# A Fourier filter and a two-layer block on one core: who begins stage one's stores, when the transform's steps are issued, and who casts the filtered product

## The chip, the cores and the metric

The kernel runs on one core of one Trainium2 chip. The metric is the device time of one execution in microseconds (us), the median of several runs.

## The reference, cut to what matters

```python
# x 8 x 3008 x 256, filt_r and filt_i 1505 x 256, w_in 256 x 2048, w_out 2048 x 256, all fp32
X = np.fft.rfft(x, axis=1)
y = np.fft.irfft(X * (filt_r + 1j * filt_i), n=3008, axis=1)
t = y.reshape(24064, 256)
h = t @ w_in
g = h * (1.0 / (1.0 + np.exp(-1.702 * h)))
out = g @ w_out
```

Each of the 8 batches goes through a Fourier transform of length 3008, a product with a filter and the transform back; its 3008 tokens then go through two matrix products with a gelu between them.

## The kernel before, in words

**Two jobs run side by side.** The two matrix products (the MLP, `mlp`, L590) of batch b keep TensorE busy; between their matmuls the transform of batch b + 1 (`fft`, L439) is done. The first transform is done alone ahead of everything, by other code that the change leaves alone. So there are seven transforms beside MLPs: the "first transform" below is the one of batch 1, done beside the MLP of batch 0; the last batch's MLP runs alone.

**The MLP.** A batch has six tiles of tokens, 512 wide; the sixth of batches 0, 2, 4 and 6 is 384 wide, since what is left over goes to the next batch. A tile has 16 chunks, one for each 128 of the 2048 middle columns, so a batch has 96 chunks. A chunk is 6 matmuls into h (L603: values are split into a high and a low part, and three products of the parts are taken, for two halves of the inner dimension) and 6 into o (L625). Between them ScalarE takes the gelu of h rounded (gh, L606) and again unrounded in place (h, L607), and VectorE takes the difference (gl, L608). gh and gl have three buffers each, h two. When a tile is done ScalarE and VectorE copy o out (L631, L634) and SyncE begins the store (L644).

**The transform, stage one** is 12 steps, two halves u of six chunks c. SyncE begins the load of x (512 KB, L444, by the helper at L182); per half ScalarE casts the high part xh (L449), GpSimd takes the low part xl (L450), TensorE does three matmuls (L279 to L281), ScalarE casts ah (L454), VectorE takes al (L455). After the second half four stores of 256 KB each (L460) bring ah and al to DRAM (a_d). x, ah, al, and later b and br, share one pool of seven buffers ("raw"), so the load of x for chunk c + 2 takes the buffer that al of chunk c - 1 leaves when its stores have landed.

**Stage two** is two empty steps and then 17 pairs, a forward step i (L493) and a backward step i - 1 (L511). Forward: two matmuls s from zy (L483 to L488), which GpSimd has loaded from a_d (L469); ScalarE copies one half and VectorE adds the other (L436, L437); VectorE multiplies by the filter (L427 to L429) and GpSimd adds (L430); then the sum c_buf is split again: VectorE casts the high part into zy (L504, twice, 48 x 512) and GpSimd takes the low part (L505, twice). Backward: two matmuls i, the halves again, and two stores of b to DRAM (b_d, L520), begun by ScalarE. From b_d come the loads br (SyncE, L182) for the last piece, which makes the tile's y: eight matmuls (L576), ScalarE's cast (L584) and VectorE's difference (L585).

**What sets the order.** The main loop (L684 to L720) walks over the chunks; behind each chunk's work it issues steps of the next transform. There are 48 calls for a batch, spread evenly over its chunks by count: the k-th is issued when 48 x chunk // chunks reaches k, where chunks is 86 (the last ten chunks of a batch get none; in batch 0 the first 16 don't either, so it is 70). The last ones are needed before the next batch's first tile is made. From the code as issued, a scheduler with a simulated clock sets the order of instructions on each engine. Each engine then runs its list strictly in that order, and a DMA is begun by the engine named, in that engine's order: a DMA that waits holds up what stands behind it there.

Of the kernel before, what the change touches and what calls it, by code (L numbers as in the profile page):

```python
# [20 lines left out]
P = 128  # L21
Q = 112
NFC = DFF // P
STEPS = 48

LEAST = 2.0**-15
MOST = float(np.uint32(0x47EFFFFF).view(np.float32))
# [125 lines left out]
def tile_kernel(  # L153
# [9 lines left out]
    nc = tc.nc  # L163
# [8 lines left out]
    def raw(name):  # L172
        return sb.tile([P, 4, D], F32, tag="raw", name=name, bufs=7)
# [6 lines left out]
    def load_in(dst, src):  # L180

        ins = nc.sync.dma_start(dst, src)  # L182
        if in_order[0]:
            tc.keep_in_program_order(ins)
# [254 lines left out]
    def fft(b):  # L439

        a_d = dram.tile([2, 48, 64, D], F32, tag="a_d", name=f"a_d{b}")
        for c in range(6):
            xr = raw(f"x_{b}_{c}")
            load_in(xr, x[b, c])  # L444
            ah, al = (sb.tile([P, 4, D], F32R, tag="raw", name=f"a{n}_{b}_{c}", bufs=7) for n in "hl")
            for u in range(2):
                xh, xl = half(f"xh_{b}_{c}_{u}"), half(f"xl_{b}_{c}_{u}")
                src = xr[:, 2 * u : 2 * u + 2, :]
                nc.scalar.copy(xh, src)  # L449
                nc.gpsimd.tensor_tensor(xl, src, xh.bitcast(F32), ALU.subtract)  # L450
                ps = ps_f.tile([P, 2, D], F32, tag="f", name=f"s1_{b}_{c}_{u}")
                mm3(ps, t1_sb[:, 0], t1_sb[:, 1], xh, xl)
                su = slice(2 * u, 2 * u + 2)
                nc.scalar.copy(ah[:, su], ps)  # L454
                nc.vector.tensor_tensor(al[:, su], ps, ah[:, su].bitcast(F32), ALU.subtract)  # L455
                yield
            for j in range(2):
                n = NH * j + 4 * c
                for k, a in enumerate((ah, al)):
                    nc.scalar.dma_start(  # L460
                        a_d[k, n : n + 4].rearrange("n k d -> k n d"), a[64 * j : 64 * j + 64].bitcast(F32)
                    )

        b_d = dram.tile([48, 64, D], F32, tag="b_d", name=f"b_d{b}")

        def load(i):
            for k in range(2):
                src = a_d[k].rearrange("n (k s) d -> n k s d", k=2)[:, :, 2 * i : 2 * i + 2, :]
                nc.gpsimd.dma_start(  # L469
                    zy[0][64 * k : 64 * k + 48, i % 2].rearrange("p k s d -> p k (s d)"),  # L470
                    src.rearrange("n k s d -> n k (s d)"),
                )

        def load_f(i):
            for k in range(2):
                load_in(f_buf[64 * k : 64 * k + 48, 2 * (i % 2) : 2 * (i % 2) + 2], fs[i])

        def second(i, m, src, name):

            ps = [ps_f.tile([P, 2, D], F32, tag="f", name=f"{name}_{b}_{i}_{k}") for k in range(2)]  # L480
            for k in range(2):
                if i == 0:
                    ins = nc.tensor.matmul(ps[k][:, 0], de_sb[:, k, m + 1], src[:, k, 0], start=True, stop=True)  # L483
                    if k == 0:
                        tc.keep_in_program_order(ins)
                    nc.tensor.matmul(ps[k][:, 1], de_sb[:, k, m], src[:, k, 1], start=True, stop=True)
                else:
                    ins = nc.tensor.matmul(ps[k], de_sb[:, k, m], src[:, k], start=True, stop=True)  # L488
                    if k == 0:
                        tc.keep_in_program_order(ins)  # L490
            return ps

        def forward(i):  # L493

            ps = second(i, 0, zy[0][:, i % 2], "s2")
            if i + 2 < 16:
                load(i + 2)
            u1 = c_buf[i % 3]
            halves(ps, u1)
            product(i, u1, u1, f_buf[:Q, 2 * (i % 2) : 2 * (i % 2) + 2])  # L500
            y = zy[0][:, 2 + i % 2]
            for k in range(2):
                h, o = slice(64 * k, 64 * k + 48), slice(64 - 64 * k, 112 - 64 * k)
                nc.vector.tensor_copy(y[h, k], u1[h])  # L504
                nc.gpsimd.tensor_tensor(y[o, k], u1[h], y[h, k].bitcast(F32), ALU.subtract)  # L505
            if i + 2 < 16:
                load_f(i + 2)

        bes = {}

        def backward(i):  # L511
            g, u = divmod(i, 2)
            if u == 0:
                bes[g] = raw(f"b_{b}_{g}")
            ps = second(i, 2, zy[0][:, 2 + i % 2], "i2")
            halves(ps, bes[g][:Q, 2 * u : 2 * u + 2, :])
            if u == 1:
                be = bes.pop(g)
                for k in range(2):
                    nc.scalar.dma_start(b_d[:, 32 * k + 4 * g : 32 * k + 4 * g + 4, :], be[64 * k : 64 * k + 48])  # L520

        for i in range(2):
            load(i)
            load_f(i)

        for i in range(2):
            yield
        for i in range(17):
            if i < 16:
                forward(i)  # L530
                yield
            if i:
                backward(i - 1)
                yield
        b_of[b] = b_d
# [148 lines left out]
    for n, (i, fc) in enumerate(turns):  # L684
        b, t = tiles[i]
        if n % (6 * NFC) == 0:

            lead = 16 if b == 0 else 0
            done, chunk, chunks = 0, 0, 6 * NFC - lead - 10
            nxt = fft(b + 1) if b + 1 < B else iter(())  # L690
        if n == 0:
            run(start(*tiles[1]))
        if n + 1 < len(turns):
            ahead(*turns[n + 1])
        chunks_of[i][1](fc, turns[n + 1 : n + 2] == [(i, fc + 1)])
        if fc == 1:
            store()
        if n < 26:
            run(conv, 1)
            if n % 2 and n < 12:  # L700
                load_unit(EARLY + 9 + n // 2)
        if n == 11:
            split_de()
            in_order[0] = False
        if n == 26:
            zy.append(const.tile([P, 4, 2, 2, D], F32R, tag="zy", name="zy"))
            nc.gpsimd.memset(zy[0].bitcast(F32), 0.0)
        if b or n >= lead:
            chunk += 1
            while chunk <= chunks and done < STEPS * chunk // chunks:  # L710
                run(nxt, 1)
                done += 1
        at = () if i == 0 else (10, 11, 13) if i == 1 else (9, 12, 13) if t == 5 else (1, 3, 9)
        if fc in at and i + 1 < len(tiles):
            if i + 1 not in sigs:
                sigs[i + 1] = start(*tiles[i + 1])
            run(sigs[i + 1], 1)
            if fc == at[-1]:
                run(sigs[i + 1])
# [29 lines left out]
```

## Time and profile before

| what | value |
|---|---|
| three runs | 2384.24, 2385.23, 2387.87 us; median 2385.23 |
| the profiled execution | 2385.31 us, of which the profile's span is 2383.5 and 1.8 lie around it |
| TensorE | 2365.1 us busy, 99% of the span, 11102 matmuls |
| VectorE, ScalarE, GpSimd | 59%, 55%, 30% busy |
| TensorE's granted clock | full speed in every slice |

PE is TensorE, DVE VectorE, ACT ScalarE, POOL GpSimd, SP SyncE; a q behind a name is the engine's sequencer, which issues DMAs. The span is the profiled execution on the chip; busy time doesn't count the issuing of DMAs. Matmuls overlap and their ends are modelled, so the distance between starts is the safer reading: a matmul of 512 columns starts every 0.227 us. The difference between span and busy time of TensorE, 18.4 us, is all the idle time that the trace shows for it.

### The profile page before, as it was taken

To read this page: it belongs to the slowest core of one execution; us is meant where nothing else is said; L and a number is where in the kernel's file an instruction comes from. 1 tells how busy PE (TensorE), PEld (TensorE's weight loads), DVE (VectorE), ACT (ScalarE), POOL (GpSimd) and SP (SyncE) were. 2 spreads that over 40 slices of the span, in tenths; PEclk is the share of its full clock that TensorE was granted. 3 is DMA by queue.
4 is the path that set the end of the run, shared out by engine and by line. 5 is a ranking of instruction groups with operands and counts; after the bars stand their busy time and mean duration, and the time that the engine had idled before them with its cause. 6 is when DMAs were issued, how large, how long until landed. Compare 5 with 4: busy or idle time off the path is not lost.

```text
span 2383.5 us, 31272 instructions
## 1 busy us (share of the span) xinstructions
PE 2365.1 (99%) x11102; PEld 1984.1 (83%) x11102; DVE 1411.2 (59%) x2199; ACT 1314.4 (55%) x2430; POOL 724.9 (30%) x675
## 2 busy tenths in 40 slices
PE   9999999999999999999999999999999999999999
PEld 7878888888888889888888888988888888898887
DVE  7967873577535774367743677437773377723222
ACT  6655655566555565555645556555654555644443
POOL 3024532344213441244412444124440144300000
PEclk9999999999999999999999999999999999999999
DMA  9255534544245442544425444354433544220000
GB/s 343 81 149 116 119 93 116 142 107 111 54 128 135 104 111 80 139 109 111 99 81 133 110 109 102 93 138 108 119 89 87 133 108 120 75 64 9 18 9 18
DMA packets 141483, 248.66 MB, mean 104 GB/s; under 512 B 15376, under 2 KB 81040, under 8 KB 141328
## 3 DMA queue, kind: packets, MB, share of 16 engines
q1 hardware_dynamic: 63088, 136.18, 19.6%
q10 hardware_dynamic: 53152, 66.44, 11.0%
q0 software_dynamic: 25088, 44.05, 9.6%
q8 instruction: 88, 1.44, 0.3%
q14 instruction: 67, 0.55, 0.1%
HBM read 152.76 MB, written 93.85 MB: 103 GB/s over the span
## 4 chain that ended last, share of the span: by engine, by line
PE 92%; DVE 3%; DMA 2%; issue 1%; ACT 1%; ACTq 0%; POOL 0%; SPq 0%; POOLq 0%; DVEq 0%
PE h L603 41%; PE o L625 41%; PE i L576 3%; PE i L488 2%; PE s L488 2%; PE s L279 1%; PE s L281 1%; PE s L280 1%; DVE u_buf L427 1%; PE s L358 1%; DVE u_buf L428 0%; DVE gl L608 0%; DMA x<-in_x_dram 0%; DVE c_buf L437 0%; DMA zy<-a_d 0%
## 5 line engine op out<-in xcount | busy, mean ns | idle before, releaser
L603 PE MATMUL h<-y,wi 128*128 128x512 f32 (+1 forms) x4608 | 1156.7, 386 | 5.7 <-DVE gl L608 5.6
L603 PEld LDWEIGHTS h<-y,wi 128*128 128x128 f32 x4608 | 854.9, 188 | 172.5 <-DVE gl L608 11.5
L608 DVE TENSOR_TENSOR gl<-h,gh 128x512 fp32r<-128x512 f32 (+1 forms) x768 | 522.3, 680 | 759.3 <-ACT h L607 746.4
L606 ACT ACTIVATE gh<-h 128x512 fp32r<-128x512 f32 (+1 forms) x768 | 453.1, 590 | 783.2 <-PE h L603 756.6
L625 PE MATMUL o<-gh,wo 128*128 128x512 f32 (+1 forms) x3072 | 821.3, 387 | 2.6 <-ACT gh L606 2.5
L625 PEld LDWEIGHTS o<-gh,wo 128*128 128x128 f32 x3072 | 569.9, 188 | 111.9 <-ACT gh L606 4.9
L625 PE MATMUL o<-gl,wo 128*128 128x512 f32 (+1 forms) x1536 | 472.5, 385 | 0.0
L607 ACT ACTIVATE h<-h 128x512 f32<-128x512 f32 (+1 forms) x768 | 448.2, 584 | 0.0
L505 POOL TENSOR_TENSOR zy<-c_buf,zy 48x512 fp32r<-48x512 f32 x224 | 314.5, 1404 | 84.0 <-DVE zy L504 74.8
L625 PEld LDWEIGHTS o<-gl,wo 128*128 128x128 f32 x1536 | 286.9, 188 | 54.9 <-DVE gl L608 0.2
L430 POOL TENSOR_TENSOR c_buf<-c_buf,u_buf 112x512 f32<-112x512 f32 x127 | 163.6, 1288 | 395.3 <-DVE c_buf L429 395.3
L450 POOL TENSOR_TENSOR xl<-x,xh 128x512 fp32r<-128x512 f32 x84 | 108.8, 1303 | 548.9 <-ACT xh L449 543.3
L469 POOL DMA_DIRECT2D zy<-a_d x224 | 129.8, 581 | 271.0 <-PE s L488 92.5
L437 DVE TENSOR_TENSOR c_buf<-s,c_buf 48x512 f32<-48x512 f32 x224 | 154.3, 689 | 33.2 <-ACT c_buf L436 28.3
L437 DVE TENSOR_TENSOR b<-i,b 48x512 f32<-48x512 f32 x224 | 154.1, 688 | 9.1 <-ACT b L436 3.6
L436 ACT COPY b<-i 48x512 f32<-48x512 f32 x224 | 130.4, 582 | 47.1 <-PE i L488 37.6
L436 ACT COPY c_buf<-s 48x512 f32<-48x512 f32 x224 | 130.5, 582 | 44.7 <-PE s L488 37.2
L576 PEld LDWEIGHTS i<-tab,br 128*128 128x128 f32 x768 | 103.1, 191 | 10.4 <-issue 1.2
L504 DVE CAST zy<-c_buf 48x512 fp32r<-48x512 f32 x224 | 96.8, 432 | 22.3 <-POOL c_buf L430 14.7
L576 PE MATMUL i<-tab,br 128*128 128x128 f32 x768 | 104.4, 274 | 1.2 <-DMA br<-b_d 1.0
L455 DVE TENSOR_TENSOR al<-s,ah 128x512 fp32r<-128x512 f32 x84 | 58.0, 690 | 69.8 <-ACT ah L454 67.6
L585 DVE TENSOR_TENSOR y<-i,y 128x512 fp32r<-128x512 f32 (+2 forms) x104 | 65.2, 632 | 40.3 <-ACT y L584 39.4
(94 smaller groups left out, 1155.0 us busy)
## 6 DMA issues: line engine op xcount, KB each, us to landing
f_buf<-fs SPq DMA_DIRECT2D x224, 192.0 KB, 3.2
zy<-a_d POOLq DMA_DIRECT2D x224, 192.0 KB, 3.6
x<-in_x_dram SPq DMA_DIRECT2D x47, 512.0 KB, 4.9
out_dram<-out SPq DMA_DIRECT2D x43, 512.0 KB, 3.6
a_d<-ah ACTq DMA_DIRECT2D x84, 256.0 KB, 3.7
a_d<-al ACTq DMA_DIRECT2D x84, 256.0 KB, 4.0
b_d<-b ACTq DMA_DIRECT2D x112, 192.0 KB, 2.5
br<-b_d SPq DMA_DIRECT2D x84, 256.0 KB, 4.4
```

Source lines behind the costliest of these rows:

```text
L430: eng.tensor_tensor(u1, u1, u2, ALU.add)
L436: nc.scalar.copy(dst[h], ps[k][o])
L437: nc.vector.tensor_tensor(dst[h], ps[k][h], dst[h], ALU.add)
L450: nc.gpsimd.tensor_tensor(xl, src, xh.bitcast(F32), ALU.subtract)
L469: nc.gpsimd.dma_start(zy[0][64 * k : 64 * k + 48, i % 2].rearrange("p k s d -> p k (s d)"), src.rearrange("n k s d -> n k (s d)"),)
L505: nc.gpsimd.tensor_tensor(y[o, k], u1[h], y[h, k].bitcast(F32), ALU.subtract)
L576: ins = nc.tensor.matmul(ps[:, P * i : P * i + P], br[m][:, i], t2_sb, start=True, stop=True)
L603: nc.tensor.matmul(ps[:, :w], wi_sb[half][:, wk, kc, c], y[:, yk, kc, :w], start=n == 0, stop=n == 5)
L606: nc.scalar.activation(gh[:, :w], ps[:, :w], AF.Gelu_apprx_sigmoid)
L607: nc.scalar.activation(ps[:, :w], ps[:, :w], AF.Gelu_apprx_sigmoid)
L608: nc.vector.tensor_tensor(gl[:, :w], ps[:, :w], gh[:, :w].bitcast(F32), ALU.subtract)
L625: nc.tensor.matmul(pos[m][:, :w], wb[:, P * m : P * m + P], g[:, :w], start=first_one, stop=last_one)
```

## The change

Three things are changed.

The four stores of a chunk of stage one (L460) are begun by SyncE instead of ScalarE.

The steps of the transform get a cost each, instead of all counting the same: 0.8 for each of the 12 of stage one, 1.3 for the two empty ones, 1.0 for the other 33, in sum 45.2. The chunks get a weight too, 4 for a chunk of a 512-wide tile and 3 for one of a 384-wide tile, and the last ten units of four get no step as before. A step is issued when the costs up to and with it are no more than the passed share of the weights. By this rule, in the MLPs of batches 1, 3 and 5 the last step of stage one is issued at chunk 19 (before at 22), the first forward step at 26 (27) and the last step at 86 (85); in those of batches 2, 4 and 6 the last step comes at chunk 83 instead of 85.

The cast of the filtered product's high part (L504) goes from VectorE to ScalarE.

```diff
--- before.py
+++ after.py
@@ -21,7 +21,7 @@
 P = 128
 Q = 112
 NFC = DFF // P
-STEPS = 48
+COSTS = [0.8] * 12 + [1.3] * 2 + [1.0] * 33
 
 LEAST = 2.0**-15
 MOST = float(np.uint32(0x47EFFFFF).view(np.float32))
@@ -457,7 +457,7 @@
             for j in range(2):
                 n = NH * j + 4 * c
                 for k, a in enumerate((ah, al)):
-                    nc.scalar.dma_start(
+                    nc.sync.dma_start(
                         a_d[k, n : n + 4].rearrange("n k d -> k n d"), a[64 * j : 64 * j + 64].bitcast(F32)
                     )
 
@@ -501,7 +501,7 @@
             y = zy[0][:, 2 + i % 2]
             for k in range(2):
                 h, o = slice(64 * k, 64 * k + 48), slice(64 - 64 * k, 112 - 64 * k)
-                nc.vector.tensor_copy(y[h, k], u1[h])
+                nc.scalar.copy(y[h, k], u1[h])
                 nc.gpsimd.tensor_tensor(y[o, k], u1[h], y[h, k].bitcast(F32), ALU.subtract)
             if i + 2 < 16:
                 load_f(i + 2)
@@ -686,7 +686,9 @@
         if n % (6 * NFC) == 0:
 
             lead = 16 if b == 0 else 0
-            done, chunk, chunks = 0, 0, 6 * NFC - lead - 10
+            widths = [3 if k // NFC == 5 and b % 2 == 0 else 4 for k in range(lead, 6 * NFC)]
+            passed, whole = 0, sum(widths) - 40
+            steps, spent = list(COSTS), 0.0
             nxt = fft(b + 1) if b + 1 < B else iter(())
         if n == 0:
             run(start(*tiles[1]))
@@ -706,10 +708,10 @@
             zy.append(const.tile([P, 4, 2, 2, D], F32R, tag="zy", name="zy"))
             nc.gpsimd.memset(zy[0].bitcast(F32), 0.0)
         if b or n >= lead:
-            chunk += 1
-            while chunk <= chunks and done < STEPS * chunk // chunks:
+            passed += widths.pop(0)
+            while steps and spent + steps[0] <= sum(COSTS) * passed / whole + 0.01:
                 run(nxt, 1)
-                done += 1
+                spent += steps.pop(0)
         at = () if i == 0 else (10, 11, 13) if i == 1 else (9, 12, 13) if t == 5 else (1, 3, 9)
         if fc in at and i + 1 < len(tiles):
             if i + 1 not in sigs:
```

SyncE in stage one of the third transform (beside the MLP of batch 1; the number behind x, ah and al is the chunk c), before:

```order
L182 DMA x_2_3618<-in_x_dram 128x1024
L182 DMA x_3_3725<-in_x_dram 128x1024
L182 DMA x_4_3830<-in_x_dram 128x1024
L644 DMA out_dram<-out_0_3805 256x1x512
L182 DMA br_2_3874<-b_d_1681 64x4x256 x2
L182 DMA x_5_3917<-in_x_dram 128x1024
```

and with the change:

```order
L182 DMA x_2_3600<-in_x_dram 128x1024
L460 DMA a_d_3424<-ah_1_3520 64x4x256 x2
L460 DMA a_d_3424<-al_1_3521 64x4x256 x2
L182 DMA x_3_3689<-in_x_dram 128x1024
L460 DMA a_d_3424<-ah_2_3602 64x4x256 x2
L460 DMA a_d_3424<-al_2_3603 64x4x256 x2
L182 DMA x_4_3771<-in_x_dram 128x1024
L460 DMA a_d_3424<-ah_3_3691 64x4x256 x2
L460 DMA a_d_3424<-al_3_3692 64x4x256 x2
L182 DMA x_5_3858<-in_x_dram 128x1024
L644 DMA out_dram<-out_0_3823 256x1x512
L460 DMA a_d_3424<-ah_4_3773 64x4x256 x2
```

Each load of x now stands behind the four stores of the chunk two before it, where before the loads followed each other; the last load has moved ahead of the tile's output store and of br.

VectorE at a forward step of stage two, before (s_2_4 is that step's matmul result, b_1 a backward step's):

```order
L428 TENSOR_TENSOR u_buf_82<-c_buf_80,f_buf 48x512
L427 SCALAR_TENSOR_TENSOR u_buf_82<-c_buf_80,f_buf 48x512
L608 TENSOR_TENSOR gl_2_9_4485<-h_2_9_4477,gh_2_9_4484 128x512
L429 TENSOR_TENSOR c_buf_80<-c_buf_80,f_buf 112x512
L608 TENSOR_TENSOR gl_2_10_4503<-h_2_10_4495,gh_2_10_4502 128x512
L504 CAST zy<-c_buf_80 48x512 x2
```

and ScalarE at a forward step with the change:

```order
L606 ACTIVATE gh_3_1_4709<-h_3_1_4702 128x512
L607 ACTIVATE h_3_1_4702<-h_3_1_4702 128x512
L520 DMA b_d_3970<-b_2_4604 48x1024
L504 CAST zy<-c_buf_79 48x512 x2
L520 DMA b_d_3970<-b_2_4604 48x1024
L606 ACTIVATE gh_3_2_4727<-h_3_2_4720 128x512
L607 ACTIVATE h_3_2_4720<-h_3_2_4720 128x512
L436 COPY c_buf_80<-s_2_7_0_4739 48x512
L436 COPY c_buf_80<-s_2_7_1_4740 48x512
L606 ACTIVATE gh_3_3_4770<-h_3_3_4763 128x512
L607 ACTIVATE h_3_3_4763<-h_3_3_4763 128x512
```

The pair of casts left VectorE, where it stood behind the next gl, and stands in ScalarE's list between pairs of gelus, here between the two stores of b.

TensorE at the end of the first transform, in the 384-wide sixth tile of batch 0 (i_1_15 is the last backward step, the second number of h the chunk of the tile), before:

```order
L488 MATMUL i_1_15_1_3139<-zy,de_sb 128x512
L625 MATMUL o_5_0_3052<-gh_5_9_3227,wo_981 128x384
L625 MATMUL o_5_1_3053<-gh_5_9_3227,wo_981 128x384
L625 MATMUL o_5_0_3052<-gh_5_9_3227,wo_981 128x384
L625 MATMUL o_5_1_3053<-gh_5_9_3227,wo_981 128x384
L603 MATMUL h_5_11_3260<-y_5_2626,wi_980 128x384 x6
```

and with the change:

```order
L488 MATMUL i_1_15_0_3083<-zy,de_sb 128x512
L603 MATMUL h_5_5_3148<-y_5_2656,wi_580 128x384 x6
L625 MATMUL o_5_0_3077<-gl_5_3_3120,wo_581 128x384
L625 MATMUL o_5_1_3078<-gl_5_3_3120,wo_581 128x384
L488 MATMUL i_1_15_1_3084<-zy,de_sb 128x512
L625 MATMUL o_5_0_3077<-gh_5_4_3137,wo_581 128x384
L625 MATMUL o_5_1_3078<-gh_5_4_3137,wo_581 128x384
L625 MATMUL o_5_0_3077<-gh_5_4_3137,wo_581 128x384
L625 MATMUL o_5_1_3078<-gh_5_4_3137,wo_581 128x384
L603 MATMUL h_5_6_3166<-y_5_2656,wi_580 128x384 x6
```

The last backward step's second matmul moved from ahead of chunk 11 of that tile to ahead of chunk 6.

## Rows read from the trace of the kernel before

**Rows 1.** The head of the page (busy us of each engine, share of the span, instructions) and, of its 40 slices, the row with TensorE's granted clock in tenths of full speed.

```profile
PE 2365.1 (99%) x11102; PEld 1984.1 (83%) x11102; DVE 1411.2 (59%) x2199; ACT 1314.4 (55%) x2430; POOL 724.9 (30%) x675
...
PEclk9999999999999999999999999999999999999999
```

**Rows 2.** The windows view: stretches of the span (us), their length, then for each engine its busy time and, in brackets, its instructions; at the end granted clock, DMA share and GB/s.

```profile
120.00:200.00 80.00, 76.27 (x349) 61.33 (x348) 51.13 (x77) 45.45 (x86) 22.66 (x20) 1.00 0.56 143
...
300.00:360.00 60.00, 55.41 (x296) 50.23 (x295) 42.32 (x67) 32.83 (x67) 23.52 (x20) 1.00 0.36 93
...
705.00:730.00 25.00, 25.00 (x116) 20.84 (x115) 9.60 (x14) 13.71 (x26) 4.39 (x4) 1.00 0.54 148
...
931.00:932.00 1.00, 0.77 (x4) 0.45 (x4) 0.00 (x0) 1.00 (x3) 1.00 (x1) 1.00 0.00 0
...
1325.00:1330.00 5.00, 3.78 (x19) 2.91 (x19) 1.98 (x3) 2.52 (x5) 1.11 (x2) 1.00 0.59 70
...
2100.00:2383.50 283.50, 278.99 (x1288) 233.44 (x1286) 79.58 (x120) 117.64 (x220) 0.53 (x2) 1.00 0.05 16
```

**Rows 3.** The waits of TensorE over the whole span: who waited for whom, us in total, times, longest.

```profile
PE h L603 <- DVE gl L608: 5.6, 9, 2.1
PE o L625 <- ACT gh L606: 2.5, 3, 2.0
PE s L483 <- DMA zy<-a_d: 2.0, 2, 1.2
...
PE i L576 <- DMA br<-b_d: 1.0, 1, 1.0
```

**Rows 4.** The first row of the waits of all engines, same columns.

```profile
ACT gh L606 <- PE h L603: 756.6, 693, 3.1
```

**Rows 5.** Groups of the page: line, engine, operation, tiles, shape, count | busy us, mean ns of one | idle time of the engine before them and what ended most of it.

```profile
L505 POOL TENSOR_TENSOR zy<-c_buf,zy 48x512 fp32r<-48x512 f32 x224 | 314.5, 1404 | 84.0 <-DVE zy L504 74.8
...
L436 ACT COPY c_buf<-s 48x512 f32<-48x512 f32 x224 | 130.5, 582 | 44.7 <-PE s L488 37.2
...
L504 DVE CAST zy<-c_buf 48x512 fp32r<-48x512 f32 x224 | 96.8, 432 | 22.3 <-POOL c_buf L430 14.7
```

**Rows 6.** The page's DMA issues: KB of one, median us from issue to landing.

```profile
x<-in_x_dram SPq DMA_DIRECT2D x47, 512.0 KB, 4.9
...
a_d<-ah ACTq DMA_DIRECT2D x84, 256.0 KB, 3.7
a_d<-al ACTq DMA_DIRECT2D x84, 256.0 KB, 4.0
```

**Rows 7.** Timeline of ScalarE in the first transform's stage one: start us, us, engine (ACTq is its sequencer issuing DMAs), line, operation, how many in a row, and idle time before with its releaser.

```profile
147.00 1.25 ACTq L460 DMA_DIRECT2D a_d<-ah  x2
148.29 1.82 ACTq L460 DMA_DIRECT2D a_d<-al  x2
150.16 0.60 ACT L606 ACTIVATE gh<-h 128x512 fp32r<-128x512 f32 x1 [3.19 <-issue]
```

**Rows 8.** Timeline of TensorE there and 11 us later, same columns.

```profile
150.81 1.19 PE L625 MATMUL o<-gh,wo 128*128 128x512 f32 x4 [2.03 <-ACT gh L606]
...
161.84 0.50 PE L279 MATMUL s<-xh,t_sb 128*128 128x512 f32 x1 [0.84 <-ACT xh L449]
```

**Rows 9.** Timeline of ScalarE in the second batch's MLP, while the third transform's stage one runs: the end of chunk 1 and the first cast of chunk 3.

```profile
389.42 0.58 ACT L454 CAST ah<-s 128x512 fp32r<-128x512 f32 x1
...
392.12 1.23 ACTq L460 DMA_DIRECT2D a_d<-al  x1
...
399.33 0.62 ACT L449 CAST xh<-x 128x512 fp32r<-128x512 f32 x1 [0.73 <-PE s L280]
```

**Rows 10.** Timeline of ScalarE, the two longest waits for an x load: one in a tile of 512 tokens, one in a tile of 384.

```profile
721.60 0.62 ACT L449 CAST xh<-x 128x512 fp32r<-128x512 f32 x1 [2.31 <-DMA x<-in_x_dram]
...
930.17 1.14 ACT L449 CAST xh<-x 128x512 fp32r<-128x512 f32 x2 [2.19 <-DMA x<-in_x_dram]
931.22 0.48 ACT L606 ACTIVATE gh<-h 128x384 fp32r<-128x384 f32 x1
```

**Rows 11.** Timeline of TensorE beside the second of them.

```profile
931.01 0.51 PE L625 MATMUL o<-gl,wo 128*128 128x384 f32 x2
931.76 0.98 PE L625 MATMUL o<-gh,wo 128*128 128x384 f32 x4 [0.23 <-ACT gh L606]
```

**Rows 12.** Timeline of VectorE near the end of the first transform.

```profile
327.83 0.69 DVE L428 TENSOR_TENSOR u_buf<-c_buf,f_buf 48x512 f32<-48x512 f32 x1
...
334.59 1.67 DVE L428 TENSOR_TENSOR u_buf<-c_buf,f_buf 48x512 f32<-48x512 f32 x1
336.28 1.65 DVE L427 SCALAR_TENSOR_TENSOR u_buf<-c_buf,f_buf 48x512 f32<-48x512 f32 x1
```

**Rows 13.** Timeline of GpSimd in the same stretch.

```profile
334.25 3.13 POOL L505 TENSOR_TENSOR zy<-c_buf,zy 48x512 fp32r<-48x512 f32 x2 [2.39 <-DVE zy L504]
```

**Rows 14.** Timeline of TensorE at chunk 32 of the third batch's MLP (the shape of it returns in each of six batches).

```profile
756.29 0.28 PE L486 MATMUL i<-zy,de_sb 128*128 128x256 f32 x1
756.89 1.45 PE L603 MATMUL h<-y,wi 128*128 128x512 f32 x5 [0.32 <-DVE gl L608]
```

**Rows 15.** Timeline of GpSimd and TensorE between stage one and stage two of the sixth transform.

```profile
1321.65 2.25 POOL L469 DMA_DIRECT2D zy<-a_d  x4 [15.02 <-issue]
...
1327.55 0.36 PE L483 MATMUL s<-zy,de_sb 128*128 128x256 f32 x1 [1.22 <-DMA zy<-a_d]
```

## The prediction

> **What bounds the kernel now.** Read the head of the page first [rows 1]: TensorE is busy for 2365.1 of 2383.5 us at full clock in every slice, with VectorE at 59%, ScalarE at 55% and GpSimd at 30%. The change adds no matmul and takes none away, so nothing can be won but TensorE's idle time, 18.4 us in all. The windows view tells where that lies [rows 2]: 80.00 - 76.27 = 3.7 us in 120 to 200 (stage one of the first transform), 60 - 55.41 = 4.6 us in 300 to 360 (that transform's end), 1.2 us in 1325 to 1330, 0.2 us at 931, and 283.50 - 278.99 = 4.5 us at the program's end, which no part of the change touches. The waits of TensorE name the releasers [rows 3]: gl of VectorE 5.6 us in 9 places, gh of ScalarE 2.5, a load of zy 2.0, a load of br 1.0. So there are a dozen short stalls, each with a cause of its own, and the sum has to be made stall by stall. The other way round, ScalarE waits 756.6 us in 693 places for TensorE's h [rows 4], 1.1 us a chunk: work that is added to or taken from ScalarE is hidden unless more than that comes at once.
>
> The whole is measured against the profiled execution, 2385.31 us, 0.08 above the median of 2385.23. About 4.8 us, 0.2%, is what a measurement can tell from no change.
>
> **Stores from SyncE: what is taken away.** In the first transform ScalarE sits in the four issues from 147.00 to 150.11 and the gh behind them begins at 150.16 [rows 7]; TensorE is idle for 2.03 us before it takes that gh [rows 8]. This stall goes: -2.0. Beside it stand 0.84 us at 161.84 for an xh that came late [rows 8] and a first wait for zy of 0.8 (the rest of the 2.0 in [rows 3], of which 1.2 is at 1327). The same group of issues in later batches, 390.0 to 393.35 [rows 9], delays no matmul: a gh can be ordered between two issues there. So 18 us of issuing that ScalarE loses per batch is worth nothing elsewhere; the cover is ScalarE's 1.1 us a chunk.
>
> The Trainium skill says in "DMA: Bandwidth & Descriptors", section "Issuing engines are not separate DMA queues", that DMAs begun by different engines run on the same 16 DMA engines, and that another issuer saves only the sequencer's time, usually small against the transfer. By that alone this term would be 0 and the whole 2 us worse. The trace disagrees here: 3.1 us of issuing made a stall of 2.03 [rows 7, 8], against a transfer of 3.7 to 4.0 us [rows 6].
>
> **Stores from SyncE: what is added.** The load of x for chunk c + 2 now stands behind four stores that wait for al of chunk c. Take chunk 1 of the third transform [rows 9]: the cast of ah ends at 390.0; four issues take 3.3 us; then x has to land. The median from issue to landing is 4.9 us [rows 6], so x is there 8.2 us after the cast; if a load alone on the queue is as quick as the stores' 3.7, 7.0. Before, x was wanted 9.3 us after that cast (399.33 - 390.00 [rows 9]). Now the steps come closer: one each 0.8 x 86 / 45.2 = 1.52 chunks instead of 86 / 48 = 1.79. At 2.72 us a chunk (12 matmuls of 0.227) that is 0.73 us per step, 1.5 us per chunk of the transform; it is wanted 7.9 us after the cast. The wait on ScalarE is so between nothing and 0.3, and where the load meets the stores' traffic, an output store or br, up to 3. What does a wait of ScalarE cost TensorE? In a 512-wide tile the longest in the trace, 2.31 us [rows 10], has no stall behind it: TensorE is busy for all of 705 to 730 [rows 2]; in a 384-wide tile 2.19 us [rows 10] costs 931.76 - 931.01 less two starts of 0.173, 0.4 us, and 0.2 in the matmuls behind it [rows 11]. I take 0.7 us for one load in each of batches 1, 3 and 5, where the steps come closest: +2.1, between 0 and 5.4 (3 x 1.8, a wait of over 3 less its cover). In the even batches the positions hardly move: 0.
>
> In the first transform's own stage one the same chain meets the tile boundary: the last x stands behind an output store, and y's cast of tile 2 stands behind xh on ScalarE, with eight matmuls waiting for it. Before, this stretch had 3.7 us of stalls [rows 2]. I put the new ones, without the 2.0 that goes, at 5.1 against 1.7, +3.4, by two more waits like the 0.84 and one of 1.7 at the boundary, an estimate between that and the 2.03. The net of the stretch is +1.4, between -2.0 and +4.
>
> **Steps by the chunks' time.** Three stalls hang on when steps come. (1) The end of the first transform, 4.6 us [rows 2]: there forward and backward steps are crowded into the narrow tile, where a chunk has 2.08 us (12 x 0.173) instead of 2.72. By the new weights the last step comes five chunks sooner, ahead of chunk 6 of that tile instead of chunk 11, and the densest part falls in 512-wide chunks. The loads br follow sooner too (1.0 of the 4.6 [rows 3]). In its place comes the first load of x of the next batch, in a narrow tile like the one at 931 [rows 10, 11]: I leave 0.8 for it and 0.4 for the rest. Net -3.4, between -4.1 and 0. (2) The stall of 1.22 us at 1327.55 for a load of zy [rows 15], whose issue on GpSimd came only at 1321.65. With stage one over three chunks sooner and the first forward step one sooner, there are two chunks, 5.4 us, more for stores and loads: -1.2, between -1.2 and 0. (3) The x wait in the narrow tiles at 931 and its like in batch 4, 0.9 together by the starts: -0.5, between -0.9 and +0.5.
>
> **The cast on ScalarE.** VectorE loses 224 casts of 432 ns, 96.8 us [rows 5]. Nearest on ScalarE is the copy of the same shape, 582 ns [rows 5]; 224 of them add 130 us to 1314, hidden under its waits for h [rows 4]. A pair takes 1.2 us in ScalarE's list between gelus, about the 1.1 us that it has free in a chunk, and far under the 2.31 that stalled nothing [rows 10]: 0, between -0.5 and the third rival's price. VectorE's relief is worth something at one place per batch: at chunk 32 the matmul behind 756.29 should start 0.12 us later, and starts 0.6 later [rows 14], for a gl that is late. At 334 to 338 one sees why: beside GpSimd's pair of L505 (3.13 us [rows 13]) VectorE's products take 1.67 and 1.65 us instead of 0.69 [rows 12]. The pair of casts ahead of them (0.87 us) is gone now, so gl comes sooner by more than the 0.5 that it was late: 6 x -0.48 = -2.9, between -2.9 and 0.
>
> **Sum.** +1.4 + 2.1 - 3.4 - 1.2 - 0.5 + 0 - 2.9 = -4.5. From 2385.3: **2380.8 us**, 0.19% less. All low ends together give -11.1 (2374), all high ends +9.9 (2395); taken as independent of each other (root of the squares of the distances) 2377 and 2387.
>
> **Rivals.** *All of it is gained.* The x chain has cover enough and the first stage one loses its 2.0 and gets nothing new: -2.0 + 0 - 4.1 - 1.2 - 0.9 + 0 - 2.9 = -11.1, 2374. For it speaks that the order was made with a simulated clock that knew of the new positions; against it, that the same clock left the stalls of before.
>
> *Given back.* The x chain costs its upper ends (+4, +5.4), the gains stand at about two thirds (-5.5): +3.9, 2389, no change that could be told. For it speaks the 7.9 us against 8.2.
>
> *The loads of x are really served after the stores: slower.* If a load on SyncE's queue starts moving only when the four stores ahead of it have, it lands 3.3 + 4.0 + 3.7 = 11.0 us after the cast [rows 6, 9], 3.1 us later than wanted. It decides from a wait of 2.3 us on [rows 10]: each of the four loads behind stores in each of six batches then costs 0.8, +19, less 8 won elsewhere: +11, 2396. Against it speaks that stores and loads of two queues overlapped so far, so that bandwidth was there; but no row has a load behind stores in one queue. The Trainium skill's page "DMA: Bandwidth & Descriptors", section "Queues, rings and completion order", says that each DMA engine takes the descriptors of a ring in ring order and goes round between rings by packets: by that rule x loses its turn beside the stores and gets one after them, which is this rival. No row of before shows it.
>
> *The cast blocks ScalarE.* It now waits for GpSimd's sum in ScalarE's own list, ahead of gh. If of the 112 forward steps each costs 0.2 us of TensorE, +22, less 8: +14, 2399. It decides where the sum is over 1.1 us late; VectorE waited there only 14.7 us in all [rows 5], which speaks against it.
>
> That the change doesn't do what it says is out: the lists of instructions show all three parts.
>
> **How the numbers follow.** Forecast (2377 to 2385) 0.42, all gained (under 2377) 0.25, given back (2385 to 2390) 0.17, loads after stores 0.10, blocked ScalarE 0.06. Half of the forecast's case lies over 0.2% under before: faster 0.21 + 0.25 = 0.46; slower, the two last rivals, 0.16; between, 0.38. The range 2373 to 2391 leaves out the two last rivals and a little below.
>
> **What would show it.** In the changed kernel's trace: no stall near 148 behind issues; SyncE's list with x about 3 us behind the first store, and ScalarE's waits for x of 0 to 3 us, with stalls of TensorE only where they pass 2.3; no stall at 1327 and none at chunk 32; the window of the first transform's end with under 2 us of idle time; ScalarE some 130 us busier, VectorE 97 less. The forecast is wrong if the waits for x pass 2.3 us in most batches (then the stores hold up the loads), or if TensorE waits for gh in many forward steps.

## The result, and the profile after

The changed kernel takes **2397.76 us** (median of 6 runs, 2396.05 to 2399.87) against 2385.44 before, a ratio of 1.0052, 95% interval 1.0039 to 1.0064. It is slower by 12.3 us; 2380.8 was forecast, with a range up to 2391. The profiled execution, one of the two longest of the six, has a span of 2397.7 us, 14.2 more than before.

Where the time went can be counted from the traces: the time from the first h matmul of one batch to that of the next (batch 0 from the span's start, batch 7 to its end), in us, here with all the experiments told below. S stands for the stores on SyncE, C for the new costs and weights, K for the cast on ScalarE. Each row but for its last column is one execution of that kernel, and one execution shows a batch to some 2 us (the last section has the reason).

| kernel | parts | 0 | 1 | 2 | 3 | 4 | 5 | 6 | 7 | span | median of runs |
|---|---|---|---|---|---|---|---|---|---|---|---|
| before | none | 361.5 | 294.8 | 286.6 | 295.2 | 287.9 | 295.1 | 286.4 | 275.9 | 2383.5 | 2385.4 |
| changed | S, C, K | 362.4 | 301.8 | 285.7 | 299.3 | 285.5 | 301.0 | 286.1 | 275.9 | 2397.7 | 2397.8 |
| E1 | C, K | 365.3 | 294.8 | 285.7 | 294.8 | 290.4 | 294.8 | 286.3 | 275.9 | 2388.0 | 2391.2 |
| E2 | S | 356.9 | 294.8 | 286.6 | 295.2 | 286.3 | 295.2 | 286.4 | 275.9 | 2377.3 | 2380.0 |
| E3 | K | 368.4 | 294.3 | 286.8 | 294.6 | 287.5 | 294.7 | 286.1 | 275.9 | 2388.3 | 2389.6 |
| E4 | C | 361.8 | 295.2 | 285.6 | 295.2 | 291.2 | 295.2 | 286.9 | 275.9 | 2387.0 | 2388.4 |
| E5 | S, K, C without the closer stage one | 362.6 | 295.2 | 285.6 | 295.2 | 285.6 | 295.2 | 285.9 | 275.9 | 2381.2 | 2383.4 |
| E6 | S, C, K, ah sooner | 361.9 | 294.9 | 285.1 | 294.9 | 287.2 | 294.8 | 286.2 | 275.9 | 2380.8 | 2384.6 |
| E7 | S, C | 358.0 | 300.6 | 285.3 | 298.7 | 285.5 | 301.3 | 287.0 | 275.9 | 2392.4 | 2394.0 |
| E8 | S, K but for the first transform | 358.4 | 295.1 | 286.7 | 294.6 | 286.2 | 294.7 | 286.1 | 275.9 | 2377.7 | 2378.2 |
| E9 | K, without its wait in the first transform | 358.4 | 294.9 | 286.6 | 295.1 | 287.3 | 294.6 | 286.1 | 275.9 | 2378.8 | 2380.5 |
| E10 | E6 with K but for the first transform | 357.7 | 294.8 | 285.1 | 294.8 | 287.5 | 294.9 | 286.1 | 275.9 | 2376.9 | 2379.5 |

The changed kernel loses 7.0 + 4.1 + 5.9 = 17.0 us in batches 1, 3 and 5, and 0.9 in batch 0; it wins 3.6 in batches 2, 4 and 6. Of the 17.0 some 10 are idle time of TensorE (11.1 us in these three batches, 0.9 before), and some 5 come from two stretches at a lower clock, at 419 and at 1595. Its windows, to be held against [rows 2] (same columns):

```profile
120.00:200.00 80.00, 76.45 (x344) 61.97 (x343) 52.66 (x79) 48.13 (x90) 29.55 (x26) 0.98 0.57 150
200.00:300.00 100.00, 97.33 (x447) 79.22 (x446) 78.28 (x112) 73.95 (x132) 52.22 (x52) 1.00 0.47 112
300.00:360.00 60.00, 58.36 (x307) 52.67 (x306) 37.23 (x55) 37.22 (x74) 19.76 (x16) 1.00 0.30 80
419.00:430.00 11.00, 7.78 (x23) 5.84 (x22) 3.66 (x6) 5.78 (x11) 2.55 (x2) 0.69 0.50 150
440.00:640.00 200.00, 200.00 (x914) 166.33 (x913) 129.87 (x191) 134.45 (x240) 80.04 (x81) 1.00 0.41 97
...
1030.00:1330.00 300.00, 300.00 (x1377) 249.84 (x1376) 165.82 (x244) 187.19 (x337) 97.60 (x96) 1.00 0.42 106
1330.00:1570.00 240.00, 240.00 (x1148) 205.58 (x1147) 141.94 (x214) 154.35 (x284) 84.77 (x81) 1.00 0.40 102
...
1595.00:1600.00 5.00, 4.53 (x13) 3.58 (x14) 3.09 (x5) 3.28 (x7) 1.33 (x2) 0.66 0.53 159
```

Read them from the bottom: from 1030 to 1570 and from 440 to 640 TensorE has no idle time at all, so the stalls at chunk 32 [rows 14] and the one at 1327 [rows 15], whose place is now 11 us later, are gone. The end of the first transform has 1.6 us of idle time instead of 4.6, but the 100 us ahead of it have 2.7 instead of none. And at 419 to 430, in batch 1, there is a hole of 3.2 us and a granted clock of 0.69. The waits of TensorE and of ScalarE name its kind, to be held against [rows 3, 4]:

```profile
PE h L603 <- DVE gl L608: 12.4, 8, 3.2
PE o L625 <- ACT gh L606: 3.0, 4, 1.3
```

```profile
ACT gh L606 <- PE h L603: 624.1, 554, 2.8
...
ACT xh L449 <- DMA x<-in_x_dram: 72.7, 25, 6.2
```

ScalarE waited for loads of x 24.9 us in 13 places before, 2.3 at most; now 72.7 in 25, 6.2 at most. What it waits for in batch 1 is seen in its timeline (the first casts of x of chunks 2 to 5, the cast that ends ah of chunk 2, and what follows the last two):

```profile
386.54 0.62 ACT L449 CAST xh<-x 128x512 fp32r<-128x512 f32 x1 [2.50 <-DMA x<-in_x_dram]
...
397.60 0.62 ACT L449 CAST xh<-x 128x512 fp32r<-128x512 f32 x1 [4.04 <-DMA x<-in_x_dram]
...
399.64 0.58 ACT L454 CAST ah<-s 128x512 fp32r<-128x512 f32 x1
...
408.59 0.62 ACT L449 CAST xh<-x 128x512 fp32r<-128x512 f32 x1 [4.60 <-DMA x<-in_x_dram]
409.12 0.59 ACT L606 ACTIVATE gh<-h 128x512 fp32r<-128x512 f32 x1
409.61 0.59 ACT L607 ACTIVATE h<-h 128x512 f32<-128x512 f32 x1
410.12 0.60 ACT L449 CAST xh<-x 128x512 fp32r<-128x512 f32 x1
410.63 0.58 ACT L454 CAST ah<-s 128x512 fp32r<-128x512 f32 x1
...
420.44 0.62 ACT L449 CAST xh<-x 128x512 fp32r<-128x512 f32 x1 [6.23 <-DMA x<-in_x_dram]
420.97 0.59 ACT L606 ACTIVATE gh<-h 128x512 fp32r<-128x512 f32 x1
```

and in SyncE's:

```profile
411.24 2.28 SPq L460 DMA_DIRECT2D a_d<-ah  x2
413.62 1.36 SPq L460 DMA_DIRECT2D a_d<-al  x2
415.08 0.98 SPq L182 DMA_DIRECT2D x<-in_x_dram  x1
```

This is **a closed loop**. ScalarE's list has the cast of x of chunk 4 (408.59) ahead of ah of chunk 3 (410.63). The stores of chunk 3 wait for that ah (411.24), the load of x of chunk 5 stands behind them on SyncE (415.08), and ScalarE waits for it until 420.44. One turn takes 11.1, 11.0 and 11.9 us between the four casts, while the steps now come a chunk every 9.8 us (in E1, which has the same steps and no late load, the casts of chunks 2 to 5 lie between 386.85 and 416.38); so each turn is later than the one before: 2.5, 4.0, 4.6, 6.2 us. TensorE pays 0.4 us at the third and 3.2 at the fourth:

```profile
418.08 1.52 PE L603 MATMUL h<-y,wi 128*128 128x512 f32 x6
422.82 2.93 PE L603 MATMUL h<-y,wi 128*128 128x512 f32 x6 [3.22 <-DVE gl L608]
425.55 1.05 PE L625 MATMUL o<-gh,wo 128*128 128x512 f32 x2
```

The gh that stands behind the cast (420.97) is late, gl after it, and TensorE idles for 3.2 us. Then the six matmuls of h take 2.93 us instead of 1.52: the granted clock is at the lower of its two levels until 428.5, and of these 5.7 us some 2.7 are lost by that (0.43 us from start to start instead of 0.227).

Batches 2, 4 and 6 of the same execution are the other half of the evidence. There a chunk comes every 8.3 to 10.4 us, no less close, and the same four stores stand ahead of each load of x; yet from chunk 1 on no load is waited for more than 0.5 us, and TensorE has no idle time. What differs is ScalarE's list: up to chunk 2 ah of a chunk stands ahead of the next chunk's x, so the loop is open. In batch 2, the end of ah of chunk 1 and the casts of x of chunk 2, then the cast of x of chunk 5:

```profile
687.03 0.59 ACT L454 CAST ah<-s 128x512 fp32r<-128x512 f32 x1 [0.83 <-PE s L281]
...
689.47 1.12 ACT L449 CAST xh<-x 128x512 fp32r<-128x512 f32 x2
...
716.07 0.62 ACT L449 CAST xh<-x 128x512 fp32r<-128x512 f32 x1 [0.38 <-DMA x<-in_x_dram]
```

### The profile page after: what moved, and what is told of

Same layout as the page of the kernel before. It is cut to its first block, busy times and chain, and to the rows that moved or that the text cites. A ratio compares the mean times of both kernels' runs of the same rounds, so it can differ in the third digit from the quotient of the medians.

```text
span 2397.7 us, 31241 instructions
## 1 busy us (share of the span) xinstructions
PE 2371.9 (99%) x11102; PEld 1986.2 (83%) x11102; DVE 1319.3 (55%) x1975; ACT 1446.0 (60%) x2654; POOL 701.2 (29%) x675
## 4 chain that ended last, share of the span: by engine, by line
PE 85%; DMA 1%; DVE 1%; ACT 1%; SPq 0%; issue 0%; ACTq 0%; DVEq 0%
PE h L603 38%; PE o L625 38%; PE i L576 3%; PE i L488 2%; PE s L488 2%; DMA x<-in_x_dram 1%; PE s L280 1%; PE s L279 1%; PE s L281 1%; SPq L460 0%; DVE gl L608 0%; ACT gh L606 0%; ACT h L607 0%; DVE u_buf L427 0%; ACT xh L449 0%
## 5 line engine op out<-in xcount | busy, mean ns | idle before, releaser
L625 PEld LDWEIGHTS o<-gl,wo 128*128 128x128 f32 x1536 | 287.5, 188 | 56.4 <-DVE gl L608 0.9
L505 POOL TENSOR_TENSOR zy<-c_buf,zy 48x512 fp32r<-48x512 f32 x224 | 291.8, 1303 | 97.7 <-ACT zy L504 83.5
L504 ACT CAST zy<-c_buf 48x512 fp32r<-48x512 f32 x224 | 138.8, 619 | 35.7 <-POOL c_buf L430 31.3
L449 ACT CAST xh<-x 128x512 fp32r<-128x512 f32 x84 | 50.3, 617 | 73.2 <-DMA x<-in_x_dram 72.7
```

The lines of the kernel that those rows point to most:

```text
L504: nc.scalar.copy(y[h, k], u1[h])
L625: nc.tensor.matmul(pos[m][:, :w], wb[:, P * m : P * m + P], g[:, :w], start=first_one, stop=last_one)
```

## The experiments

Each comparison is of runs on one chip with the kernel before, which took 2384.7 us beside E1 to E4 and 2385.4 beside the others.

**E1 to E4: the parts by themselves.** E1, from the changed kernel:

```diff
-                    nc.sync.dma_start(
+                    nc.scalar.dma_start(
```

> The changed kernel with stage one's stores begun by ScalarE again; costs and cast as changed. Theory A (closed loop: ScalarE casts the x of chunk c+2 ahead of ah of chunk c+1, the stores of c+1 wait for that ah on SyncE, and the load of x for c+3 stands behind those stores; 11.0 us a turn against 9.7 us between chunks): the loop is open, no stall of 2.5 to 3.4 us in the MLPs of batches 1, 3 and 5, TensorE at full clock there; 2379 to 2385. Rival B (the closer steps are too dense for ScalarE and the loads, whoever begins the stores): 2392 or more, with the same stalls at chunk 18 of these batches. Rival C (the casts on ScalarE): 2392 or more.

E2, from the kernel before:

```diff
-                    nc.scalar.dma_start(
+                    nc.sync.dma_start(
```

> The kernel before with only the stores moved to SyncE. Theory A: the loop is there too, but a chunk of the transform comes every 11.1 us, about the loop's 11.0 to 11.9, so waits for x on ScalarE grow to 2 us or little more by the last chunk and TensorE hardly stalls; the stall of 2.0 us at 148 is gone; 2382 to 2389. Rival D (a load behind stores on one queue is late whatever the spacing, by traffic or order of service): waits of 4 to 6 us as in the changed kernel, in all six batches, 2395 or more.

E3, from the kernel before:

```diff
-                nc.vector.tensor_copy(y[h, k], u1[h])
+                nc.scalar.copy(y[h, k], u1[h])
```

> The kernel before with only the cast of the filtered product's high part on ScalarE. Theory A: the stalls at chunk 32 of six batches go, nothing else changes; 2381 to 2385. Rival C (the casts hold up gh): 2390 or more, TensorE waiting for gh in many forward steps.

E4 has the diff's first, fourth and fifth piece alone.

> The kernel before with only the new costs and weights. Theory A: x loads stand behind no stores, so the closer steps cost nothing but a wait or two of ScalarE under 2.5 us; the first transform's end and the stall at 1327 are better; 2377 to 2385. Rival B: the stalls of the odd batches are there; 2392 or more.

Measured: E1 2391.21 (ratio 1.0024, 1.0015 to 1.0033), E2 2380.01 (0.9977, 0.9967 to 0.9987), E3 2389.61 (1.0015, 1.0006 to 1.0024), E4 2388.35 (1.0013, 1.0004 to 1.0022). The stores alone are a gain of 4.7 us, the cast alone costs 4.9, the costs alone 3.6: in sum +3.8, and the three together +12.3. The rest, 8.5 us, is made only by parts together, and the table shows where: in batches 1, 3 and 5 every one of E1 to E4 is at 294.3 to 295.2. Neither closer steps alone (E4) nor stores ahead of loads alone (E2) stall there. In E2 ScalarE waits often but shortly:

```profile
ACT xh L449 <- DMA x<-in_x_dram: 41.0, 27, 2.3
```

27 waits and none over 2.3 us: the loop is there, its turns of some 11 us no longer than the 11.1 between chunks. That takes away rivals B and D for the odd batches. But theory A's times were missed, for E1, E3 and E4 by 3 to 6 us, for E2 by 2 us the other way, so there are causes besides the loop. E3 loses 6.9 us in batch 0. E1 loses 3.8 there: the closer steps bring ScalarE's four issues (163.66 to 168.22) ahead of y's cast, TensorE waits for that, and the clock falls behind it. E4 has this stall too (2.23 us), though its batch 0 is only 0.3 longer:

```profile
168.91 0.74 PE L603 MATMUL h<-y,wi 128*128 128x512 f32 x2 [2.24 <-ACT y L584]
```

And E1 and E4 lose 2.5 and 3.3 us in batch 4, at the place of the stall in [rows 15]. There, in E1:

```profile
1318.98 1.07 PE L625 MATMUL o<-gh,wo 128*128 128x512 f32 x4
1322.91 0.36 PE L483 MATMUL s<-zy,de_sb 128*128 128x256 f32 x1 [2.86 <-DMA zy<-a_d]
```

```profile
1316.79 2.24 POOL L469 DMA_DIRECT2D zy<-a_d  x4 [10.88 <-issue]
```

GpSimd began these loads with nothing in the profile to wait for ("issue"), 2.1 us after the last of stage one's stores had landed (1314.71); the first forward step now comes sooner than they land, and the clock was at 0.76 in the 7 us after it. GpSimd begins late at this one transform in every kernel, 0.7 us after the last landing in the changed kernel, 1.1 in E7, 2.0 to 2.7 in all others; why stays open. When the first forward step is due decides the rest: the stall is missing in the changed kernel, E2, E5, E7 and E8, and 1.8 us in E6.

**E5: stage one no closer than before,** from the changed kernel:

```diff
-COSTS = [0.8] * 12 + [1.3] * 2 + [1.0] * 33
+COSTS = [1.0] * 12 + [1.3] * 2 + [1.0] * 33
```

> The changed kernel with a cost of 1.0 instead of 0.8 for stage one's steps, so that a chunk of the transform comes every 10.6 to 11.2 us again; stores by SyncE, weights by tile width and cast as changed. Theory A (loop of 11.0 us, chunks every 9.7): waits for x stay under 2.5 us, the stalls of batches 1, 3 and 5 (17 us together with the lowered clock) go; 2377 to 2383. Rival E (weights and stores together cause it in another way): 2392 or more.

**E6: the order on ScalarE,** from the changed kernel:

```diff
-                nc.scalar.copy(xh, src)
+                tc.keep_in_program_order(nc.scalar.copy(xh, src))
...
-                nc.scalar.copy(ah[:, su], ps)
+                tc.keep_in_program_order(nc.scalar.copy(ah[:, su], ps))
```

> The changed kernel with stage one's casts xh and ah kept nearer to program order on ScalarE: ah of chunks 1 and 2 now stands ahead of the xh of two chunks later, while the xh of chunks 4 and 5 still stand ahead of ah of 3 and 4 in the odd batches; stores and steps as changed, 9.7 us between chunks. Theory A: a turn of the loop is cut out, so lateness starts again at chunk 4 and reaches about 2.5 to 4 us at chunk 5 instead of 6.2: the stalls of the odd batches fall from 3.8 to 4.3 to about 1 each and the clock holds; 2382 to 2389. Rival D (x behind stores is late by itself): ScalarE's waits and the time stay, 2394 or more.

**E7: without the cast,** from the changed kernel:

```diff
-                nc.scalar.copy(y[h, k], u1[h])
+                nc.vector.tensor_copy(y[h, k], u1[h])
```

> Stores by SyncE and the new costs and weights, the cast on VectorE as before. Theory A: the loop and the closer steps are both there, so batches 1, 3 and 5 lose 4 to 7 us each as in the changed kernel, and the first transform is some 3 us better without the cast; 2392 to 2399. Rival C (the cast on ScalarE is needed for the stalls): 2382 or less.

Measured: E5 2383.39 (0.9992, 0.9984 to 1.0001), 0.4 above its range, E6 2384.55 (0.9995, 0.9986 to 1.0004), E7 2394.04 (1.0037, 1.0023 to 1.0050). Batches 1, 3 and 5 are at 295.2 in E5, at 294.8 to 294.9 in E6, at 298.7 to 301.3 in E7. Each way of opening the loop, by time between chunks, by the order of two casts, or by the stores' queue (E1), takes the loss of the odd batches away whole; taking the cast away does nothing there. With the even batches above, that shows the loop to be the cause of what these batches lose. The waits of ScalarE in E6 and in E7:

```profile
ACT xh L449 <- DMA x<-in_x_dram: 10.4, 7, 2.9
```

```profile
ACT xh L449 <- DMA x<-in_x_dram: 71.4, 24, 7.2
```

In E6 SyncE's list has the loads behind the stores as in the changed kernel, and the steps are as close; lateness starts again at chunk 4 and reaches 1.9 us at chunk 5 in batch 1, less than the 2.5 to 4 expected. So a load behind four stores isn't late by itself; it is late where ScalarE waits for it before it makes what those stores wait for.

**E8: the cast in all transforms but the first, with E2's stores,** from E2:

```diff
-                nc.vector.tensor_copy(y[h, k], u1[h])
+                (nc.scalar.copy if b > 1 else nc.vector.tensor_copy)(y[h, k], u1[h])
```

> The kernel before with the stores on SyncE, and the cast on ScalarE in all transforms but the first (there on VectorE); steps as before. Theory A with the cast's loss lying in the first transform alone (E3: batch 0 6.9 us longer, each later batch 0.5 shorter): the 2380.0 of the stores alone less 6 x 0.5, 2376 to 2379. Rival C (the cast costs everywhere): 2382 or more.

**E9: the cast without its wait,** from E3:

```diff
-                nc.scalar.copy(y[h, k], u1[h])
+                nc.scalar.copy(y[h, k], u1[h] if b > 1 else f_buf[h, 2 * (i % 2)])
```

> E3 (only the cast on ScalarE), but in the first transform the two casts read the filter's buffer instead of the sum, so they take ScalarE's time without waiting for GpSimd's sum; what the first transform gives is left out by that. Theory C1 (the wait for the sum, ahead of gh in ScalarE's list, makes the 6.9 us that batch 0 loses in E3): batch 0 back to 361 to 364 us, the whole 2381 to 2385. Theory C2 (the 1.2 us of casts per step are too much for ScalarE there): batch 0 stays at 366 or more, the whole at 2388 or more.

Measured: E8 2378.16 (0.9970, 0.9958 to 0.9981), E9 2380.51 (0.9978, 0.9969 to 0.9987). E8 came out as expected, but the 3 us over E2 aren't shown: the ratios, 0.9970 and 0.9977, have intervals that overlap, and the spans are alike; batches 3 and 5 are 0.6 and 0.5 shorter, batch 0, where nothing was changed, is 1.5 longer (a fall of the clock, told in the last section). E9 has all casts on ScalarE, and batch 0 takes 358.4 instead of E3's 368.4, below the 361 to 364 of theory C1; ScalarE's waits for the sum are, in E3 and in E9:

```profile
ACT zy L504 <- POOL c_buf L430: 29.5, 54, 3.0
```

```profile
ACT zy L504 <- POOL c_buf L430: 16.9, 45, 0.6
```

So the time that the casts take isn't what hurts. That it is their wait is shown only in part. E9 also frees the scheduler to place the casts elsewhere (the first stands at 152.0 instead of 201.5), so it takes away wait and place together. In E3's own trace 1.5 of the 6.9 us are stalls of TensorE for a gh that stands behind a cast's wait, 0.65 us at 260.76 and 0.81 at 278.34. The second, on ScalarE and then on TensorE:

```profile
275.92 0.63 ACT L504 CAST zy<-c_buf 48x512 fp32r<-48x512 f32 x1 [1.43 <-POOL c_buf L430]
...
277.69 0.60 ACT L606 ACTIVATE gh<-h 128x512 fp32r<-128x512 f32 x1
```

```profile
278.34 1.20 PE L625 MATMUL o<-gh,wo 128*128 128x512 f32 x4 [0.81 <-ACT gh L606]
...
281.33 1.66 PE L603 MATMUL h<-y,wi 128*128 128x512 f32 x6 [1.57 <-DVE gl L608]
```

Another 3.4 us are two stretches at the lower clock, one of them at 152, ahead of the first cast on ScalarE. The rest, stalls for gl like the one at 281.33 among it, isn't settled. Nor does a long wait always cost: in the changed kernel the cast waits 2.87 us at 288.87, but TensorE's stall of 1.48 us lies ahead of that, and the h behind it starts without idle time. On ScalarE and then on TensorE:

```profile
288.87 1.26 ACT L504 CAST zy<-c_buf 48x512 fp32r<-48x512 f32 x2 [2.87 <-POOL c_buf L430]
290.15 0.60 ACT L606 ACTIVATE gh<-h 128x512 fp32r<-128x512 f32 x1
```

```profile
286.86 1.65 PE L603 MATMUL h<-y,wi 128*128 128x512 f32 x6 [1.48 <-DVE gl L608]
...
290.30 1.64 PE L603 MATMUL h<-y,wi 128*128 128x512 f32 x6
```

**E10: both places mended,** from the changed kernel: E6's edit in all transforms but the first, and E8's choice of engine for the cast.

> The changed kernel with the two places mended: in all transforms but the first, xh and ah kept nearer to program order on ScalarE as in E6; in the first transform the cast on VectorE. By the batches of E6, E7 and E8, theory A gives 358 + 3 x 294.9 + 285.1 + 287.2 + 286.2 + 275.9 = 2377 for the span, 2375 to 2381 for the time. If the parts don't add up so (another rival cause in batch 0 or batch 4): 2383 or more.

Measured: 2379.52 (0.9974, 0.9964 to 0.9985), span 2376.9 against the 2377 summed from the batches of E6, E7 and E8. It is the change with its gains left, 18 us faster than the change and 0.26% faster than before. E8, with fewer parts, is as fast, and E2's interval (0.9967 to 0.9987) overlaps theirs: of the three parts only the stores' move is shown to win time.

## Why the prediction was wrong

**The step that failed** is the added wait: "I take 0.7 us for one load in each of batches 1, 3 and 5 ...: +2.1, between 0 and 5.4". These batches lost 17.0 us. Under this term two things were wrong, and a third was missing.

The first is a reading. "x was wanted 9.3 us after that cast (399.33 - 390.00 [rows 9])" takes the cast at 399.33 for the first of chunk 3, as [rows 9] calls it. It is the second half's, and was released by a matmul (PE s L280) and not by a load. The first half's, which needs the load, stands 3.5 us ahead of it, in the kernel before:

```profile
395.83 0.63 ACT L449 CAST xh<-x 128x512 fp32r<-128x512 f32 x1
```

So x was wanted 5.8 us after the cast of ah and not 9.3. With the steps closer it is 4.9 and not 7.9, as E4 shows, where no store stands ahead of the load:

```profile
387.39 0.58 ACT L454 CAST ah<-s 128x512 fp32r<-128x512 f32 x1
...
392.86 0.61 ACT L449 CAST xh<-x 128x512 fp32r<-128x512 f32 x1
```

The way from the cast of ah to the landed x, put at 8.2 us, was right: 8.4 us in three of the four turns (400.22 to 408.59 is one), 9.2 in the last. A load was so late by some 3 us and not by 0.3, before any loop, and beyond the 2.3 us from which the prediction itself let TensorE pay.

The second is the overlap: I took each load by itself and let it begin on time. In the list of [rows 9] the first cast of x of chunk 3 (395.83) stands ahead of the end of ah of chunk 2, whose stores now hold up the next load. So lateness is handed on, 0.6 to 1.6 us a turn, up to 6.2. Missing altogether was the lowered clock behind a stall, some 5 of the 17.0 us.

That the even batches would cost nothing was right by luck. "The positions hardly move" does not hold: by the new weights the last step of stage one is issued at chunk 18 instead of 22 there, closer than in the odd ones (19). What spares them is the order of ScalarE's list, which no term looked at. A slip beside it: all low ends of the terms together give -11.6, not -11.1, since the cast's own -0.5 was left out.

The rival *loads after stores* had the right place, sign and point of decision (2.3 us) and came to 2396, at a chance of 0.10; its mechanism was wrong. It had the stores' data hold up the load's, so that x lands 11.0 us after the cast; it landed after 8.4. The page's DMA issues of the changed kernel, to be held against [rows 6], give

```profile
x<-in_x_dram SPq DMA_DIRECT2D x47, 512.0 KB, 5.1
...
a_d<-ah SPq DMA_DIRECT2D x84, 256.0 KB, 3.5
a_d<-al SPq DMA_DIRECT2D x84, 256.0 KB, 3.8
```

From its issue a load of x lands after 5.1 us, before 4.9, and the stores are no slower: what is late is the issue, which stands behind issues that wait. The ring order of the Trainium skill's "DMA: Bandwidth & Descriptors", section "Queues, rings and completion order", is so not what made this time.

**The cast at 0** was wrong in the first transform: E7 against the changed kernel is 4.4 us better in batch 0, and E3 6.9 worse than before. The bound from [rows 10], 2.31 us of wait that stalls nothing, held for the wait at 288.87 and failed for E3's of 1.43 us at 275.92: what a wait costs hangs on when TensorE wants the gh behind it. *The cast blocks ScalarE* had this mechanism, but spread it over all 112 steps; how much of the 6.9 and the 4.4 us it makes is not shown.

**The net of the first stage one, +1.4,** can be seen in E2: with the stores alone batch 0 is 4.6 us shorter, so the 2.0 and most of the two waits beside it went, and nothing came back at the tile boundary. In the changed kernel 3.6 us of idle time are left in 120 to 200, about the 3.7 of before, and 0.5 in E5, whose stage one is no closer: there the closer steps cost what the stores won. A clock of 0.98 over these 80 us adds 1.6, so that the +1.4 is about met, by luck, since the clock was no part of it. The Trainium skill says ("DMA: Bandwidth & Descriptors", section "Issuing engines are not separate DMA queues") that another issuer saves only the time of initiating the DMA, "usually small relative to the DMA itself". Issue time is what moved here, but it wasn't small: four issues of 3.1 us [rows 7], against 3.7 to 4.0 for a transfer, held a gh, and E2 wins 4.7 us.

**Right:** the stalls at chunk 32 are gone with the cast (E3 has none of the six left; its batches 1, 3 and 5 are 0.4 to 0.6 us shorter; forecast 0.48). **Right by luck:** the stall at 1327 and the x wait of batch 4 are gone (batch 4 2.4 us shorter; forecast 1.2 and part of 0.5). The term took the positions of the odd batches; in batch 4 the first forward step is issued at chunk 24 instead of 27, and with the new costs alone (E4) the loads begin 8.0 us sooner, at 1313.62, and the step is due 9.5 sooner, so that the stall grows from 1.22 to 2.77 us. The end of the first transform won 3.0 at its place (forecast 3.4), and lost 2.7 in the 100 us ahead of it, which the term didn't look at.

## What to carry to other kernels

When a transfer is moved to another queue, follow the loop: what does the transfer behind it wait for, who waits for that, and does that engine's list come back to what the first transfer waits for? If it does, compare the time of a turn with the time between turns; what is missing is lost at every turn, and the cover of one wait says nothing. Take the time at which a load is wanted from the first instruction that reads it. And an instruction moved to the engine that feeds TensorE is priced by what it waits for there and where it stands, not by its duration alone.

## What the runs showed of the hardware

Short stalls of TensorE can cost twice. In the changed kernel the stall of 3.2 us at 419 is followed by matmuls 0.43 us apart instead of 0.227, the lower of the two clock levels, until 428.5; one of 2.3 us at 1007 is not. Nor does length alone decide: E3 and the kernel before have the same stall behind the four issues, 2.05 and 2.03 us, and then, in E3 and before:

```profile
152.00:156.00 4.00, 4.00 (x12) 3.15 (x11) 2.15 (x4) 1.95 (x4) 0.00 (x0) 0.57 0.00 0
```

```profile
152.00:156.00 4.00, 3.98 (x18) 3.28 (x18) 2.55 (x4) 2.55 (x6) 0.00 (x0) 1.00 0.05 15
```

A clock of 0.57 and 12 matmuls against 1.00 and 18. E2 and E8 have the same first transform, and the same stall for gl ahead of 334.3, 2.14 and 2.15 us; then, in E2 and in E8:

```profile
334.30:340.00 5.70, 5.70 (x32) 5.66 (x33) 4.22 (x8) 2.33 (x5) 4.04 (x3) 1.00 0.26 72
```

```profile
334.30:340.00 5.70, 5.70 (x23) 5.61 (x24) 3.69 (x7) 1.87 (x5) 4.01 (x3) 0.70 0.26 72
```

The fall costs 1.7 us (0.30 of 5.7), which is about what E8's batch 0 is longer. Nor is it a matter of the kernel alone: of the 31 executions of the kernel before that stand beside E1 to E4, 20 have a mean granted clock of 1.000 and spans of 2381.7 to 2383.3 us, 7 have 0.998 and 2385.3 to 2386.5. So the same instructions meet the fall in one execution and not in another, and a single trace shows a batch no finer than one such fall. What tells the two apart is not seen in the profile.
